# Attention with a gated convolution on one core: V loaded in rows of two tokens, cast by halves of the partitions, masked by a minimum per partition, in a new order of steps

## The chip, the core and the metric

The kernel runs on one core of a Trainium2 chip. The core has five engines that run side by side: TensorE (PE in the profile, its weight loads PEld), VectorE (DVE), ScalarE (ACT), GpSimd (POOL) and SyncE (SP), which here issues nearly all transfers. Sixteen DMA engines move data between the chip's memory and the core's on-chip memory of 128 partitions. The metric is the device time of one execution in microseconds (us); lower is better. Several executions are timed and their median is taken; one execution is profiled.

## What is computed

Eight sequences, eight heads of 64 features, 576 tokens. Attention is causal by blocks of 64 tokens: a query sees all keys of its own block and of those before. Its output x (heads side by side, 512 features) goes through a causal convolution of five taps into a sigmoid gate, through a matrix into values, and gate times values through a second matrix:

```python
scores = scale * np.matmul(q, k.transpose(0, 1, 3, 2))
mask = block_i >= block_j                    # blocks of 64 tokens
attn = softmax(np.where(mask, scores, -1e9))
x = np.matmul(attn, v)                       # then heads side by side
gate = 1.0 / (1.0 + np.exp(-gate_pre))       # gate_pre: conv of x, 5 taps
return gate * (x @ w_val) @ w_out
```

Inputs and output are float32; the kernel works in float16 with float32 sums.

## The kernel before

Work is cut into 32 pairs of heads, four pairs to a batch (a sequence). For each pair, q and k are loaded (L333, rows of 1 KB), cast to float16 (L416, tiles kc and qc), transposed on PE (L441, step T) and evicted into the tile kq (L449 for k, L458 for q). The last 64 tokens of all heads of a batch are a tail with loads, a transpose (L468, step U) and two evictions (L480) of their own. Scores are made with the keys on the partitions, in three steps S for each pair, and ACT takes their exponential into the tile pt (L523, 1,024 columns at a time).

A key tile has 128 keys, two blocks, on the 128 partitions, in the order of the tokens: the earlier block on partitions 0 to 63, the later on 64 to 127. For the queries of the earlier block the later keys must not count, so after the exponential `zeros` (L542) writes zeros into the upper 64 partitions of such columns, on POOL or DVE; `keep_last` (L530) copies the upper half of one block into a small tile pd, where the lower half stays zero.

V is loaded with one token of a head on a partition, 64 floats, 256 B in a row: for the first two batches head by head (L397, `load_head`), then by 128 tokens of all eight heads (L386, `load_v`). Each piece is cast by one instruction of 128x512 (L416) into the tile ve, which has a column of ones beside V for the sums of the softmax. V's tail goes to the upper 64 partitions and is cast there (tile vtail). Step P multiplies pt with ve; DVE takes the reciprocal of the sums (L573) and scales (L583, tile xn). Step X transposes xn on PE, its eviction writes xt (L606); step G is the convolution as matmuls, whose tanh is on ACT (L629); step V is the value matrix, whose product with the gate is on DVE (L651, tile gv); step O is the output matrix, evicted by ACT or DVE (L674, L676) and stored by SP (L684).

No engine's order is left to chance. PE's is a written string, `ORDER`, one letter for each of its 318 steps. For steps that may run on several engines a second string, `CHOICE`, says on which. The class `Planner` then plays the program through with durations, delays between engines and transfer rates from tables, lets each other engine take what it can start earliest, weighed by rank, and so fixes each engine's order; SP's loads of q, k and V follow a fixed list (`queue`). An instruction that waits holds up all that stand behind it on its engine. Where the planner expects PE to be idle in the first 60 us it puts in matmuls of zeros (tile nought, "fillers"). Steps of PE have a mode, by the shape of their matmuls; the planner counts a change between modes with 96 ns, and with about 120 ns an instruction on DVE or POOL that works on the upper partitions after one that does not, or the other way round.

Of the kernel before, what the change touches and what calls it, by code (L numbers as in the profile page):

```python
# [9 lines left out]
SUM_MAX = 60000.0  # L10

# [17 lines left out]
SETUP, SEEN, LANES, SLOTS, SINGLE = 1000, 1400, 8, 2048, 8  # L29

FROM, BUSY, FILL, FULL, NOUGHT = 1050, 9500.0, 60000.0, 4700, (108, 55)


WEIGH = {"PE": 0, "DVE": 83, "ACT": 69, "POOL": 127, "SP": 0}

ORDER = (
    "TTSUSSTSSSTPSSTcXSSSSPPXGPXTXUGVSSVGTGVSVSSVPSVTVPSSXTSVXSSSPGGXPUTGXTSVVGSSVVVS"
    "SVVVSTTPSSPSOXSPSXGXSTTGGSUPSSOXSPSSVVGTTVVSSSVVVVXSTTPSUPXSGGSXPSSOSXOSGGTSVVSS"
    "VVVSUTPPTSOSSVVVSXTPSSOXXGGSSOTSPPSSOXUGGTSVVXTSVVVVSSTPPSSOXSPXGGSXVVVSSTOTUVVS"
    "SSPPGGSTVVSXSVVVSSXPPSTOSSOSTOXXGGGSSTVVVVVVSSSPPPXSGGVVPXXOXGGGVVVVVVVVOOOfOO")  # L40

CHOICE = (
    "DDDADAPPPPDDDPDDDDDPAPDDDDPPPDDADPDADPPDDAAPADPDDDDPDPPDAAADDPPDDPPDADDDPDPPDAAD"
    "PPPADPPDDPPDDDDDPPPDPPPDDAAPPPPADDDDPPPPDPDADDDPDDPPDDPPPPADDPPDDPPPDDADDDDDDPPD"
    "DPDPDDPPDDDDPPDPDAADPPPDAADADPDPDPDDDDPPPPDPPAADDDPDPDDDDDDDAPPAAPDPDDADADPPDPPD"
    "DADPPPPDPDADDPPPAPPDDDPPPADPDDPDPPDDDPDDDDPPDDADPDDDDPPDDDPPDDPPDDDDDPDPPADPPPPA"
    "AAPAAPDPPDDDDPDDDDPPDADDDDDPPDDPPPPAPDADDPPDAAA")
# [15 lines left out]
class Planner:  # L63
# [40 lines left out]
    def plan(self):  # L104
# [3 lines left out]
        bank_free = [0.0] * 7 + [BUSY]  # L108
        mode, dma = None, 0.0
        lands = [0.0] * LANES  # L110
# [33 lines left out]
        def parts(s):  # L144
            rate = s.size[1]
            return s.size[0] / (256 if rate < 250 else 1024 if 300 < rate < 320 else 2048)
# [26 lines left out]
        for left in range(len(self.steps)):  # L173
# [35 lines left out]
            elif s.size:  # L209
                dma = max(dma, s.end + SETUP) + s.size[0] / s.size[1]  # L210
# [19 lines left out]
def kernel(  # L230
# [35 lines left out]
    def ring(n, shape, dtype, name):  # L266
        return [fpool.tile(shape, dtype, tag=f"{name}{i}", name=f"{name}{i}") for i in range(n)]
# [17 lines left out]
    NRAW, NVR, NC, NT, NPT, NX, NXT, NTH, NOB = 3, 5, 4, 8, 4, 3, 3, 8, 4  # L285
    UNIT, TILES = 4, 9
    raws = {n: ring(NRAW, [128, 4, 4, 64], fp32, n + "raw") for n in ("k", "q")}
    vraws = ring(NVR, [128, 8, 64], fp32, "vraw")
# [5 lines left out]
    vtail32 = ring(2, [128, 8, 64], fp32, "vtail32")  # L294
# [3 lines left out]
    KT, K0, Q0 = 128, 192, 704  # L298
# [10 lines left out]
    warm = ring(1, [128, 1], fp32, "warm")[0]  # L309
    ge, both = [raws[n][0][:, :, :, :].rearrange("p e t d -> p (e t d)")[:, 0:NP * 10]  # L310
# [52 lines left out]
    RUN = {1024: 310.0, 256: 200.0, 2048: 330.0, 0: 290.0}  # L363
# [5 lines left out]
    chunks = []  # L369
# [775 lines left out]
```

## Time and profile before

| | before |
|---|---|
| timed runs, median (lowest to highest) | 192.67 us (191.81 to 193.69) |
| the profiled execution, its own time | 193.37 us |
| its span, first to last instruction | 191.4 us |
| PE clock granted | 0.99 |
| bytes moved | 41.02 MB in 64,183 packets, 39,301 of them under 512 B |
| DMA engines' share of busy time on SP's queue | 77.3% of the span |

The span in 40 slices of 4.8 us, as the profile's page draws it (a digit is the busy share in tenths):

```profile
PE   7978999788999989999999999999999999999940
DVE  5468775685978869897989756888977786876020
ACT  3587999497788969799789889688979877743430
POOL 5224451463674615535523546142716001100000
DMA  5999999799869999969999799999981062004291
```

Read the rows against each other: DMA is full from the second slice to the thirtieth, when the last inputs have come; PE has its few gaps in the first seventeen and is full from there to the end. A transfer's price shows in the share of engine time that its packets take, an engine's wait in the idle time before an instruction and in what ended it. The wait is often put down to the engine that ran last, so the reader has to follow it back to what that engine itself had waited for.

### The profile page before, as it was taken

What the parts mean: (1) busy time and instruction counts of PE and PEld (TensorE: products, weight loads), DVE (VectorE), ACT (ScalarE), POOL (GpSimd) and SP (SyncE); (2) the same over time, 40 slices, a digit from 0 to 9 for tenths busy, and PEclk for the clock granted to TensorE, in tenths of its full rate; (3) what the DMA queues carried; (4) which work ended last, traced back from release to release, by engine and by line L of the source; (5) the groups of instructions that cost most, each with busy time, mean ns of one, the idle gap of its engine ahead of it and who ended that gap; (6) DMA issues with size and microseconds to landing.
All of it is one profiled execution on the core that took longest, in us unless ns stands there. A gap on an engine that the chain in (4) does not pass through costs nothing.

```text
span 191.4 us, 9072 instructions
## 1 busy us (share of the span) xinstructions
PE 176.8 (92%) x3898; PEld 130.3 (68%) x3898; DVE 137.6 (72%) x335; ACT 144.1 (75%) x183; POOL 69.4 (36%) x161
## 2 busy tenths in 40 slices
PE   7978999788999989999999999999999999999940
PEld 7766876566676747686686666777688568878430
DVE  5468775685978869897989756888977786876020
ACT  3587999497788969799789889688979877743430
POOL 5224451463674615535523546142716001100000
PEclk9999999999999999999999999999999999999996
DMA  5999999799869999969999799999981062004291
GB/s 152 264 284 306 216 235 340 190 272 198 255 154 263 242 295 262 255 157 322 333 225 270 190 317 288 238 279 281 270 268 47 37 207 92 3 3 113 93 305 56
DMA packets 64183, 41.02 MB, mean 214 GB/s; under 512 B 39301, under 2 KB 58757, under 8 KB 64138
## 3 DMA queue, kind: packets, MB, share of 16 engines
q1 hardware_dynamic: 63562, 39.87, 77.3%
q8 instruction: 32, 0.52, 1.2%
q10 hardware_dynamic: 576, 0.52, 0.9%
q14 instruction: 13, 0.11, 0.2%
HBM read 30.42 MB, written 9.44 MB: 208 GB/s over the span
## 4 chain that ended last, share of the span: by engine, by line
PE 65%; DMA 15%; DVE 9%; ACT 2%; issue 2%; SPq 2%; POOL 0%; ACTq 0%; DVEq 0%; POOLq 0%
PE ps L255 59%; DMA qraw<-in_q_dram 10%; PE ps L441 3%; DMA kraw<-in_k_dram 3%; PE ps L594 3%; DMA tail<-in_q_dram 2%; DVE gv L651 2%; DVE kq L449 1%; DVE w_out L416 1%; ACT kq L458 1%; DVE xn L583 1%; DVE qc L416 1%; SPq L386 1%; DVE kq L458 1%; DVE pd L530 1%
## 5 line engine op out<-in xcount | busy, mean ns | idle before, releaser
L523 ACT ACTIVATE pt<-ps 128x1024 f16<-128x1024 f32 x96 | 94.2, 1025 | 17.3 <-PE ps L255 13.8
L255 PE MATMUL ps<-xt,w_val 128*64 128x288 f16 x512 | 36.3, 288 | 0.0
L255 PE MATMUL ps<-kq 64*128 64x64 f16 (+4 forms) x448 | 33.2, 260 | 1.8 <-DVE kq L480 0.9
L255 PE MATMUL ps<-ve,pt 128*128 128x65 f16 x896 | 33.0, 193 | 1.1 <-issue 0.8
L255 PE MATMUL ps<-w_out,gv 64*128 64x512 f16 (+1 forms) x304 | 33.7, 365 | 0.0
L255 PEld LDWEIGHTS <-pt 128*128 128x128 f16 x896 | 30.1, 97 | 4.0 <-issue 2.1
L651 DVE SCALAR_TENSOR_TENSOR gv<-th,ps 128x288 f16<-128x288 f32 x64 | 27.2, 450 | 6.3 <-PE ps L255 5.3
L255 PEld LDWEIGHTS <-w_val 128*64 128x64 f16 x512 | 27.0, 110 | 5.1 <-issue 2.9
L583 DVE TENSOR_TENSOR xn<-ps,rinv 128x640 f16<-128x640 f32 x32 | 26.4, 824 | 1.1
L255 PEld LDWEIGHTS <-kq 64*128 64x128 f16 x448 | 16.0, 94 | 14.8 <-issue 5.6
L255 PE MATMUL ps<-xt,diag 64*64 64x288 f16 x640 | 23.4, 285 | 0.0
L255 PEld LDWEIGHTS <-gv 64*128 64x128 f16 x304 | 13.8, 94 | 13.2 <-issue 0.2
L629 ACT ACTIVATE th<-ps 128x576 f32<-128x576 f32 x32 | 20.1, 660 | 1.9 <-PE ps L255 1.7
L542 POOL MEMSET pt<- 64x256 f16 x41 | 13.2, 323 | 21.0 <-ACT pt L523 15.5
L255 PEld LDWEIGHTS <-diag 64*64 64x64 f16 x640 | 17.1, 106 | 2.5 <-issue 1.0
L416 POOL CAST qc<-qraw 128x512 f16<-128x512 f32 x22 | 13.6, 629 | 12.6 <-DMA qraw<-in_q_dram 12.1
L416 POOL CAST kc<-kraw 128x512 f16<-128x512 f32 x22 | 13.5, 630 | 12.7 <-DMA kraw<-in_k_dram 10.7
L449 DVE COPY kq<-ps 128x512 f16<-128x512 f16 x19 | 13.1, 690 | 6.9 <-PE ps L441 6.4
L676 DVE TENSOR_SCALAR ob<-ps 128x1024 f32<-128x1024 f32 (+1 forms) x12 | 13.1, 1090 | 3.9 <-PE ps L255 2.3
L255 PE MATMUL ps<-nought 128*128 128x128 f16 x132 | 11.8, 250 | 1.7 <-POOL nought L343 1.0
L674 ACT ACTIVATE ob<-ps 128x1024 f32<-128x1024 f32 (+1 forms) x9 | 8.0, 885 | 6.7 <-PE ps L255 6.7
L573 DVE RECIPROCAL rinv<-ps 128x10 f32<-128x10 f32 x32 | 6.9, 216 | 8.0 <-PE ps L255 7.7
(67 smaller groups left out, 207.4 us busy)
## 6 DMA issues: line engine op xcount, KB each, us to landing
kraw<-in_k_dram SPq DMA_DIRECT2D x12, 512.0 KB, 5.2
qraw<-in_q_dram SPq DMA_DIRECT2D x12, 512.0 KB, 6.5
vraw<-in_v_dram SPq DMA_DIRECT2D x24, 256.0 KB, 6.4
out_dram<-ob SPq DMA_DIRECT2D x11, 512.0 KB, 4.0
kraw<-in_k_dram SPq DMA_DIRECT2D x8, 256.0 KB, 4.3
vraw<-in_v_dram SPq DMA_DIRECT2D x16, 128.0 KB, 5.2
qraw<-in_q_dram SPq DMA_DIRECT2D x7, 256.0 KB, 5.3
out_dram<-ob SPq DMA_DIRECT2D x4, 384.0 KB, 5.7
```

What stands on the lines that cost most here:

```text
L255: nc.tensor.matmul(out=out, lhsT=lhsT, rhs=rhs, start=start, stop=stop, skip_group_check=True)
L416: copier(s.engine)(out=out, in_=in_)
L441: nc.tensor.transpose(out=o, in_=c16[name][rows, t, :, :], identity=ident16[rows, rows])
L449: copier(s.engine)(out=kqs[:, p % NT, K0:K0 + 512].rearrange("p (r s t) -> p r s t", r=2, t=4), in_=ps16[:, i:i + 2, 256:512].rearrange("p ...
L523: nc.scalar.activation(out=heads(p)[:, :, 512 * c:512 * c + 512], in_=ps[:, i:i + 2, :], func=AF.Exp, bias=0.0, scale=0.125)
L542: setter(s.engine).memset(seg[:, :, :, 0:64], 0.0)
L573: nc.vector.reciprocal(out=rinv[:, p, :, :].rearrange("p e (c x) -> p e c x", x=1), in_=o[:, :, :, 64:65])
L583: nc.vector.tensor_tensor(out=xns[p % NX][:, :, :, :].rearrange("p c e d -> p e c d"), in0=o[:, :, :, 0:64], in1=ri.to_broadcast([128, 2, ...
L629: nc.scalar.activation(out=ths[at % NTH][:, 0:n, :, :].rearrange("p n r x -> p (n r) x"), in_=ps[:, i:i + 2 * n, 0:HALF], func=AF.Tanh, bi ...
L651: nc.vector.scalar_tensor_tensor(out=gv[:, 2 * g + r, s0:s0 + HALF], in0=ths[at % NTH][:, n, r, :], scalar=1.0, in1=ps[:, va.group[0], 0:H ...
L674: nc.scalar.activation(out=o, in_=x, func=AF.Copy, bias=0.0, scale=0.5)
L676: nc.vector.tensor_scalar(out=o, in0=x, scalar1=0.5, scalar2=None, op0=ALU.mult)
```

## The change

- A row of V now has two tokens, 512 B. Partition p of a load holds tokens 2p and 2p+1 of a chunk of 256. From the third batch on a batch has two loads of 512 KB instead of four of 256 KB; the buffers are three of 512 KB instead of five of 256 KB.
- The cast puts even tokens on partitions 0 to 63 of a key tile and odd ones on 64 to 127. That takes four casts of 64 partitions for each load: the halves of the load (f) make different key tiles, the halves of the row (u) different partitions. In the first two batches a pair has two steps of two such casts, half as long. V's tail is cast by two instructions of 32 partitions.
- The two blocks of a key tile now alternate in quarters of 32 partitions. The writes that transpose and evict k follow that order. The masks become `tensor_scalar` with a minimum against one of two numbers per partition (tile keep: 65504 or 0), over all 128 partitions.
- The planner gets a rate for rows of 512 B, transfers 7% longer than before, starting times for the first transfers, other weights, and new strings `ORDER` and `CHOICE`.

```diff
-WEIGH = {"PE": 0, "DVE": 83, "ACT": 69, "POOL": 127, "SP": 0}
+WEIGH = {"PE": 0, "DVE": 101, "ACT": 144, "POOL": 117, "SP": 0}
...
-    "TTSUSSTSSSTPSSTcXSSSSPPXGPXTXUGVSSVGTGVSVSSVPSVTVPSSXTSVXSSSPGGXPUTGXTSVVGSSVVVS"
+    "TTUSSTSScSPSTSSSTXPSSPSXPXGGUGXTVGSTVSVSVSSVVSPTVVSXSTSPSSPSXGXUGPTGTXSSVVSSVVVV"
...
-        lands = [0.0] * LANES
+        lands = list(BEFORE)
...
-                dma = max(dma, s.end + SETUP) + s.size[0] / s.size[1]
+                dma = max(dma, s.end + SETUP) + SLOW * s.size[0] / s.size[1]
...
-    RUN = {1024: 310.0, 256: 200.0, 2048: 330.0, 0: 290.0}
+    RUN = {1024: 310.0, 256: 200.0, 512: 265.0, 2048: 330.0, 0: 290.0}
...
     def load_v(b, c):
-            nc.sync.dma_start(out=t[:, :, :],
-                              in_=v[b, :, 128 * c:128 * c + 128, :].rearrange("h p d -> p h d"))
+            nc.sync.dma_start(out=t[:, :, :], in_=v[b, :, 256 * c:256 * c + 256, :].rearrange(
+                "h (p u) d -> p h (u d)", u=2))
...
     def load_head(p, e):
             nc.sync.dma_start(out=t, in_=v[b, 2 * j + e, 0:512, :].rearrange(
-                "(c p) d -> p c d", p=128))
+                "(c p u) d -> p c (u d)", p=128, u=2))
...
+    def spread(key, engines, todo, needs):
+
+        def emit(s):
+            for out, in_ in todo:
+                copier(s.engine)(out=out, in_=in_)
+
+        return add("", key, engines, emit, needs)
...
     def keep_last(p):
-            copier(s.engine)(
-                out=pds[p % NPT][64:128, 0:128].rearrange("p (e x) -> p e x", e=2),
-                in_=heads(p)[64:128, :, 960:1024])
+            setter(s.engine).tensor_scalar(
+                out=pds[p % NPT][:, 0:128].rearrange("p (e x) -> p e x", e=2),
+                in0=heads(p)[:, :, 960:1024], scalar1=keep[:, 1:2], scalar2=None, op0=ALU.min)
...
     def zeros(p, first):
-            setter(s.engine).memset(seg[:, :, :, 0:64], 0.0)
+            seg = seg[:, :, :, 0:64]
+            setter(s.engine).tensor_scalar(out=seg, in0=seg, scalar1=keep[:, 0:1],
+                                           scalar2=None, op0=ALU.min)
...
-            for c in range(4) if b > 1 else ():
+            for c in range(2) if b > 1 else ():
-                chunks.append(copy_step(
-                    p - 1 + 0.1 * c, {"POOL": 613, "DVE": 430, "ACT": 600},
-                    ves[b % 2][:, :, c, 0:64], vraws[(4 * b + c) % NVR][:, :, :],
+                chunks[2 * n] = chunks[2 * n + 1] = [spread(
+                    p - 1 + 0.2 * c, {"POOL": 613, "DVE": 430, "ACT": 600},
+                    [(ves[b % 2][64 * u:64 * u + 64, :, 2 * c + f, 0:64],
+                      vraws[n % NVR][64 * f:64 * f + 64, :, 64 * u:64 * u + 64])],
...
+                    for f in range(2) for u in range(2)]
...
-            chunks.append(copy_step(
-                p - 0.9, {"POOL": 613, "DVE": 430, "ACT": 600},
+            chunks[p] = [spread(
+                p - 0.9, {"POOL": 700, "DVE": 490, "ACT": 660},
+                [(ves[b % 2][64 * u:64 * u + 64, 2 * j:2 * j + 2, f:4:2, 0:64],
+                  vraw(p)[64 * f:64 * f + 64, :, 64 * u:64 * u + 64].rearrange(
+                      "p (e c) d -> p e c d", e=2)) for f in range(2)],
+                P["lv"] + [fill["ve"]]) for u in range(2)]
```

Three places show what the strings and the planner make of it. On SP's queue, the loads of V for the fourth batch, before (tile names carry the number of their buffer, and the last figures are partitions and elements):

```order
L406 DMA vtail_101<-in_v_dram 64x8x64
L386 DMA vraw_85<-in_v_dram 128x8x64
L386 DMA vraw_86<-in_v_dram 128x8x64
L386 DMA vraw_87<-in_v_dram 128x8x64
L684 DMA out_dram<-ob_130 128x2x512
L386 DMA vraw_83<-in_v_dram 128x8x64
L333 DMA kraw_78<-in_k_dram 128x4x256
L333 DMA qraw_81<-in_q_dram 128x4x256
```

and now:

```order
L422 DMA vtail_98<-in_v_dram 64x8x64
L390 DMA vraw_83<-in_v_dram 128x8x128
L390 DMA vraw_84<-in_v_dram 128x8x128
L707 DMA out_dram<-ob_127 128x2x512
L336 DMA kraw_78<-in_k_dram 128x4x256
L336 DMA qraw_81<-in_q_dram 128x4x256
```

Two loads stand where four stood, and the store of an output tile comes behind all of V instead of ahead of its last quarter. On DVE, around the evictions of the fourth batch's tail (L480) before:

```order
L458 COPY kq_106<-ps 128x512
L449 COPY kq_106<-ps 128x512
L458 COPY kq_106<-ps 128x512
L416 COPY kq_106<-kq_106 128x64
L416 CAST ve_105<-vraw_87 128x8x64
L480 COPY kq_106<-ps 128x4x64 x2
L573 RECIPROCAL rinv<-ps 128x10
L583 TENSOR_TENSOR xn_117<-ps,rinv 128x2x5x64
```

and now (L497 and L501 are the evictions of the tail's k and q, L564 a mask, L415 a cast of V):

```order
L629 COPY xt_117<-ps 128x2x5x64
L415 CAST ve_102<-vraw_83 64x8x64
L497 COPY kq_103<-ps 128x4x2x32
L501 COPY kq_103<-ps 128x4x64
L432 COPY kq_103<-kq_103 128x2x32
L415 CAST ve_102<-vraw_84 64x8x64
L596 RECIPROCAL rinv<-ps 128x10
L606 TENSOR_TENSOR xn_114<-ps,rinv 128x2x5x64
L415 CAST ve_102<-vraw_84 64x8x64 x2
L564 TENSOR_SCALAR pt_104<-pt_104,keep_129 128x2x2x64 x2
```

In both a cast of V stands directly ahead of the two evictions; now three more follow soon. On DVE, at the first pairs, before:

```order
L416 COPY kq_106<-kq_106 128x64
L416 CAST ve_104<-vraw_83 128x8x64
L416 CAST kc_90<-kraw_78 128x2x4x64
L416 CAST qc_94<-qraw_81 128x2x4x64
L449 COPY kq_106<-ps 128x512
L458 COPY kq_106<-ps 128x512
L573 RECIPROCAL rinv<-ps 128x10
```

and now:

```order
L432 COPY kq_103<-kq_103 128x2x32
L415 CAST ve_101<-vraw_83 64x4x64 x4
L564 TENSOR_SCALAR pt_104<-pt_104,keep_129 128x2x2x64
L765 COPY convT<-ps 128x20
L432 CAST qc_92<-qraw_81 128x2x4x64
L596 RECIPROCAL rinv<-ps 128x10
```

One cast of V became four, and a mask of the first pair moved onto DVE, ahead of the cast of a later q. In all, DVE has 36 casts of V where it had 13 (20 of them short), POOL 32 for 14 and ACT 12 for 5; ten casts of q and k moved from POOL to DVE and four evictions of tails from DVE to ACT. DVE has 49 masks for 38, POOL 47 for 58. PE has 143 fillers for 132 and 132 changes of mode for 129.

More of the change, by code (lines that the diff above doesn't have):

```diff
@@ L508, in emit @@
                 group(448, 0, 6, 64, stop=False)
-                group(448, KT - 64, 8, 64, start=False)
+                group(448, KT, 8, 64, start=False)
             else:
@@ L794 @@
             done = [pairs[x]["pv"] for x in range(p - 8, p - 4)] if b > 1 else []
-            T["cv"] = copy_step(p - 0.6, {"POOL": 613}, vtails[b % 2][64:128, :, 0:64],
-                                vtail32[b % 2][64:128, :, :], [T["lv"], fill["vtail"]] + done, True)
+            T["cv"] = spread(p - 0.6, {"POOL": 1226},
+                             [(vtails[b % 2][64 * u + 32:64 * u + 64, :, 0:64],
+                               vtail32[64 * (b % 2) + 32 * u:64 * (b % 2) + 32 * u + 32, :, :]) for u in range(2)],
+                             [T["lv"], fill["vtail"]] + done)
         users = before(p - NT, "s0", "s1", "s2")
```

111 lines of the change are left out of this document (62 added, 49 removed).

## The prediction

> **What bounds the kernel now.** I read the page's busy times first, then a table of stretches of the span, then what TensorE (PE) waited for, then the time lines around the longest of those waits, and last the transfers.
>
> ```profile
> PE 176.8 (92%) x3898; PEld 130.3 (68%) x3898; DVE 137.6 (72%) x335; ACT 144.1 (75%) x183; POOL 69.4 (36%) x161
> 25.00:41.00 16.00, 14.07 (x311) 9.31 (x304) 11.19 (x30) 13.26 (x18) 6.26 (x14) 1.00 0.90 254
> 41.00:55.00 14.00, 12.91 (x300) 9.72 (x296) 10.72 (x27) 11.52 (x15) 8.97 (x20) 1.00 0.97 228
> 55.00:83.00 28.00, 26.82 (x642) 19.52 (x639) 23.05 (x56) 23.40 (x31) 13.86 (x30) 1.00 0.97 243
> 83.00:145.00 62.00, 61.77 (x1412) 44.94 (x1412) 50.89 (x117) 52.14 (x64) 26.03 (x58) 1.00 0.96 266
> 145.00:175.00 30.00, 30.00 (x690) 22.92 (x686) 22.28 (x52) 21.80 (x29) 4.55 (x13) 1.00 0.21 63
> ```
>
> A row of stretches has the stretch, its length, busy time (and count) of PE, PEld, DVE, ACT and POOL, the granted clock, the busy share of the DMA engines and GB/s. PE runs at full clock and from 83 us on is idle for 0.23 us in 92: there it is the bound, and its work is the same in both kernels. Between 25 and 83 us it is idle for 1.93 + 1.09 + 1.18 = 4.2 us, and the DMA engines are 90 to 97% busy until 145 us. So there is little to win: those 4.2 us, the fillers ahead of them, and some waits that the modelled ends of matmuls cover. Who makes them:
>
> ```profile
> PE ps L255 <- DVE kq L480: 0.9, 1, 0.9
> PE ps L441 <- DVE qc L416: 0.9, 2, 0.5
> PE ps L255 <- issue: 0.8, 1, 0.8
> PE ps L441 <- POOL kc L416: 0.8, 1, 0.8
> PE ps L441 <- DVE xn L583: 0.7, 1, 0.7
> PE ps L255 <- DVE gv L651: 0.4, 2, 0.2
> ```
>
> Columns: total us, times, longest. The engines named are mostly not the cause. The time lines at 34 and 68 us (start, duration, in brackets the idle time before and its releaser):
>
> ```profile
> 33.55 0.68 PE L255 MATMUL ps<-xt,w_val 128*64 128x288 f16 x8
> 34.98 0.63 DVE L416 CAST qc<-qraw 128x512 f16<-128x512 f32 x1 [1.30 <-DMA qraw<-in_q_dram]
> 35.02 0.29 PE L441 MATMUL ps<-ident,kc 64*128 64x64 f16 x8 [0.80 <-POOL kc L416]
> 35.67 0.29 PE L441 MATMUL ps<-ident,qc 64*128 64x64 f16 x8 [0.36 <-DVE qc L416]
> 39.23 0.29 PE L441 MATMUL ps<-ident,kc 64*128 64x64 f16 x8 [0.67 <-DVE xn L583]
> ...
> 67.72 0.43 DVE L416 CAST ve<-vraw 128x512 f16<-128x512 f32 x1 [1.28 <-DMA vraw<-in_v_dram]
> 68.07 0.75 DVE L480 COPY kq<-ps 128x256 f16<-128x256 f16 x2
> 68.87 0.64 PE L255 MATMUL ps<-kq 64*128 64x448 f16 x12 [0.92 <-DVE kq L480]
> ```
>
> DVE stands 1.30 us at a q cast whose load has not landed, and the xn step behind it makes PE wait again at 39 us. At 68 us DVE stands 1.28 us at a V cast, with the evictions of the tail behind it, for which PE waits. Late loads, not DVE's speed, make these waits.
>
> **The change, part by part.** *Rows of 512 B.* 64 heads of 512 tokens of 256 B are 8.39 MB in 32,768 packets; the change halves the packets. Three stretches in which one packet size filled the engines give the price of a packet (256 B in the last, 1 KB in the first, 2 KB in the middle):
>
> ```profile
> 2.30:4.30 2.00, 2.00 (x20) 1.82 (x18) 1.73 (x13) 1.42 (x2) 0.72 (x5) 1.00 1.00 314
> 28.00:30.00 2.00, 2.00 (x60) 1.31 (x52) 1.02 (x3) 2.00 (x5) 1.21 (x3) 1.00 0.98 355
> 44.20:46.20 2.00, 1.18 (x37) 0.97 (x32) 0.59 (x2) 1.66 (x3) 0.99 (x2) 1.00 1.09 197
> ```
>
> With 16 engines that is 16 x 256 / 197 = 20.8 ns, 16 x 1024 / 314 = 52.2 ns and 92.3 ns a packet. On the line between the first two, 512 B take 31.3 ns, 262 GB/s. V then takes 32.0 us of the engines instead of 42.6: 10.6 less, or 1.26 us for each MB (bounds: 0 at 197 GB/s, 15.9 at 314).
>
> What PE gets of it: ahead of the q load that is late at 35 us stand the heads of six pairs, 1.57 MB, so it lands 2.0 us earlier, more than the 1.30 that DVE waited. Ahead of the V load at 67.7 us stand 2.1 MB of heads and 1.8 MB of batches 2 and 3: 4.9 us, more than 1.28. Both waits go. On PE, counted from start to start against the same step undisturbed:
>
> ```profile
> 27.05 0.68 PE L255 MATMUL ps<-xt,w_val 128*64 128x288 f16 x8
> 27.66 0.81 PE L255 MATMUL ps<-xt,diag 64*64 64x288 f16 x20
> ...
> 32.21 0.60 PE L255 MATMUL ps<-ve,pt 128*128 128x65 f16 x14
> 32.67 0.59 PE L255 MATMUL ps<-ve,pt 128*128 128x65 f16 x14
> 33.22 0.39 PE L255 MATMUL ps<-kq 64*128 64x128 f16 x6
> ```
>
> A V step takes 0.61 us, at 33.55 it took 1.47 until the next: 0.86 lost. The wait at 35.67 costs another 0.36, 0.67 go at 39.23, 0.92 at 68.87, and the gv waits at 80 us (0.4) stand behind a late q cast too. The q wait at 12.5 us (0.5, the other of the two in its row) has one pair's V ahead of it, 0.3 us. Sum 0.86 + 0.36 + 0.67 + 0.92 + 0.4 + 0.3 = 3.5 us saved. The bound below is 0, the bound above the 4.2 idle plus 1.
>
> *Casts by 64 partitions.* From batch 2 on a load has four casts of 64x512 where two loads had one of 128x512 each: 48 for 24. For batches 0 and 1 a pair has four of 64x256 for one. V's tail has two of 32x512 for one.
>
> ```profile
> L416 POOL CAST ve<-vraw 128x512 f16<-128x512 f32 x14 | 8.6, 623 | 0.4
> L416 DVE CAST ve<-vraw 128x512 f16<-128x512 f32 x13 | 5.7, 446 | 1.3 <-DMA vraw<-in_v_dram 1.3
> L416 DVE CAST qc<-qraw 128x512 f16<-128x512 f32 x9 | 4.6, 507 | 3.6 <-DMA qraw<-in_q_dram 3.6
> L416 POOL CAST vtail<-vtail 64x512 f16<-64x512 f32 x8 | 5.0, 629 | 2.9 <-DMA vtail<-in_v_dram 2.0 <-PE ps L441 0.8
> L542 POOL MEMSET pt<- 64x256 f16 x41 | 13.2, 323 | 21.0 <-ACT pt L523 15.5
> L542 DVE MEMSET pt<- 64x128 uint32 x23 | 3.7, 165 | 1.8 <-ACT pt L523 1.3
> L530 DVE COPY pd<-pt 64x128 f16<-64x128 f16 x15 | 3.5, 232 | 2.3 <-ACT pt L523 2.0
> ```
>
> The vtail row shows that 64 partitions take as long as 128 (629 against 623 ns), so a halved cast saves nothing. In the new order DVE has 16 long and 20 short casts for 13: 16 x 0.446 + 20 x 0.27 (an estimate, between 0.22 and 0.446) - 5.7 = +6.8 us. Ten casts of k and q move from POOL to DVE, 10 x 0.47 = +4.7.
>
> *Masks by a minimum.* The trace has no such instruction. On DVE the nearest rows are the memset (165 ns) and the copy of pd (232): I take 200 for 29 + 20 of them, 9.8 us against 3.7 + 3.5, +2.6; at 165 it is +0.9, at the 446 of a cast +14.7. Four tail evictions move to ACT, 0.375 each by the row at 68.07, -1.5. DVE: 6.8 + 4.7 + 2.6 - 1.5 = +12.6 us. POOL has 24 long and 8 short casts of V for 14 (+9 to +10), 8 more of vtail (+5), ten of k and q fewer (-6.3), and 47 minima for 58 masks (from -3 us at a memset's 323 ns to +11 at a cast's 623): about +8 us on an engine at 36%, hidden by its idle time; if that cover is gone, the P steps wait for their masks. ACT takes seven casts and four evictions more, some 4 us on 52.14 of 62 busy in 83:145.
>
> Of these, PE pays where DVE is late without a DMA in front. In 83:145 DVE is busy for 50.9 of 62 us, 82%; a share of the 12.6 us (62 of 169 us) brings it to 89%. At 82% PE lost 0.23 us there. Bounds: 0, and 12.6 if all of it lies on the path. I take 0.8, near the lower end, since that row is the nearest.
>
> *What a rule would make of it.* Around an upper-half mask DVE's pipeline does not overlap:
>
> ```profile
> 13.43 0.69 DVE L449 COPY kq<-ps 128x512 f16<-128x512 f16 x1 [0.46 <-PE ps L441]
> 14.04 0.41 DVE L458 COPY kq<-ps 128x512 f16<-128x512 f16 x1
> 15.59 0.42 DVE L416 CAST ve<-vraw 128x512 f16<-128x512 f32 x1
> 16.04 0.19 DVE L530 COPY pd<-pt 64x128 f16<-64x128 f16 x1
> ```
>
> The second copy starts 0.08 us before the first ends, the mask 0.03 after the cast ends: 0.11 us each way. DVE has 20 runs of such masks; whole-width masks take 40 x 0.11 = 4.4 us of held time away. The Trainium skill (VectorE: DVE Perf Modes, section Two Vector instructions with no wait between them) says that an instruction is held until all earlier ones finish when its input or its output starts in another 32-partition quadrant than the last one's. By that rule the four casts of a group, which start at 0/0, 0/64, 64/0 and 64/64, are held one after the other, some 45 times here, 5 us, and give it all back; without the rule DVE's term would be +8.2 instead of +12.6, and 0.5 on PE instead of 0.8. I leave the 4.4 us out of the sum.
>
> *New order of PE.* The steps are the same. It has 132 changes of matmul mode instead of 129: the P step above takes 0.46 us for its first head and 0.55 for the second with a change behind it, so 0.1 each, +0.3. It has 143 fillers instead of 132, which stand where the plan expects PE idle:
>
> ```profile
> 15.07 1.18 PE L255 MATMUL ps<-nought 128*128 128x128 f16 x18
> ```
>
> 11 of them at 1.18 / 18 us are +0.7. SP issues two V loads a batch instead of four; behind each it comes to k and q sooner, counted above.
>
> **Sum.** -3.5 + 0.8 + 0.3 + 0.7 = -1.7 us. The profiled execution took 193.37 us (span 191.4, so 2.0 outside it), 0.7 above the median of 192.67; 193.4 - 1.7 = 191.7 there. Against the median: 191.0 us, 0.9% less.
>
> **Rivals.** *Bigger gain.* If loads that are early let PE run through 25 to 83 us without any idle time (4.2 for 3.5) and the waits that its records cover (about 1 us) and half of DVE's term go, it is -1.7 - 0.7 - 1 - 0.4 = -3.8, 188.9 us. For it: the DMA share of 0.97 there. Against: the 0.8 of "issue" is no load's.
>
> *Nothing moves.* The casts of the first pairs are four short ones on DVE, and the time won by loads is lost behind them: each group takes 4 x 0.27 against 0.446, 0.6 more, in front of the first P steps; five groups on DVE are 3 us. If half is paid, the sum is -0.2: 192.5. If the change does not do what it says, 512 B packets at 197 GB/s, the 3.5 go and the sum is +1.8: 194.5.
>
> *Slower: one load of 512 KB holds DVE's queue.* Now a cast waits for half as much. If DVE stands in front of a V load with the tail's evictions behind, as at 67.72, and does so in four of the batches 2 to 7, it costs 4 x 1.2 = 4.8 with the rest as summed: +3.1, 195.8 us. It decides from the second such wait on. For it: the order has a V cast directly ahead of both tail evictions on DVE. Against: DMA has 10 us more room.
>
> **How the numbers follow.** Forecast (faster by about 0.9%, 189.6 to 191.9): 0.45. Bigger gain 0.19, nothing moves 0.17, slower 0.19. One per cent, 1.9 us, is about what a measurement of this kernel can tell from no change. Under 190.7 fall the bigger gain and half of the forecast, 0.42; over 194.6 the slower case and little else, 0.20; between them 0.38. The range of 187.8 to 195.2 leaves out the outer part of the two end cases, under 2 in 10.
>
> **What would show it.** Right: the DVE waits for q at 35 us and V at 68 us gone, PE idle between 25 and 83 us under 2 us, loads ended near 135 us instead of 145, under 512 B some 6,500 packets; DVE near 150 us, PE's idle time in 83:145 under 1 us; the minimum at 200 ns on DVE. Wrong: new PE waits for DVE's evictions behind V casts, minima over 300 ns, or a DMA share as before until 145 us.

## The result, and the profile after

The changed kernel takes 199.62 us (median; 199.27 to 203.4) against 192.45 us of the kernel before on the same chip: a ratio of 1.034, 95% interval 1.026 to 1.041. It is slower, and outside the range that was forecast. Some executions of a kernel run a few per cent longer than its others, and the profiled one here is such (203.4 us, span 201.6, against 197.89 to 199.93 for the rest), so its rows say where the time goes, while ratios here and below are those of the other executions.

From the page of the kernel after: busy time by engine, packets, and SP's queue of transfers.

```profile
PE 179.4 (89%) x3909; PEld 131.6 (65%) x3909; DVE 152.3 (76%) x383; ACT 148.8 (74%) x194; POOL 100.9 (50%) x168
...
DMA packets 47607, 41.02 MB, mean 203 GB/s; under 512 B 6341, under 2 KB 42181, under 8 KB 47562
...
q1 hardware_dynamic: 46986, 39.86, 68.4%
```

The rows did their work: 68.4% of 201.6 us are 137.9 us of engine time on SP's queue where 77.3% of 191.4 were 148.0, so 10.1 us less (10.6 were predicted). DVE is busy for 152.3 us (150.2 predicted). POOL is busy for 100.9 us where 69.4 stood before, 31.5 more, and the prediction had written 8.

The stretches of the kernel after (busy time and count of PE, PEld, DVE, ACT, POOL, granted clock, DMA share, GB/s), and what PE waited for:

```profile
25.00:41.00 16.00, 15.07 (x352) 10.94 (x350) 14.28 (x37) 13.26 (x21) 9.75 (x18) 1.00 0.90 278
41.00:55.00 14.00, 12.12 (x296) 9.37 (x297) 12.08 (x28) 12.35 (x18) 11.55 (x17) 1.00 0.89 231
55.00:83.00 28.00, 23.47 (x508) 16.01 (x508) 20.49 (x51) 19.26 (x24) 14.61 (x23) 0.94 0.79 216
83.00:145.00 62.00, 59.42 (x1342) 42.48 (x1338) 52.27 (x120) 51.59 (x66) 41.93 (x66) 1.00 0.86 250
```

```profile
PE ps L257 <- issue: 5.0, 3, 2.6
PE ps L257 <- POOL pt L564: 2.0, 3, 0.8
PE ps L257 <- DVE kq L474: 1.3, 1, 1.3
...
PE ps L257 <- DVE xn L606: 1.0, 2, 0.5
...
PE ps L257 <- DVE pt L564: 0.6, 1, 0.6
```

Between 25 and 83 us PE is idle for 0.93 + 1.88 + 4.53 = 7.3 us where it was 4.2; from 83 to 145 for 2.58 where it was 0.23. Two kinds of wait stand on top: "issue", in which PE waits for nothing that the profile shows (0.8 us before), and the masks (L564, none before).

These sums are those of one execution. The kernel after with V's loads cut in halves takes as long (1.039, see below), and its profile, of a span of 198.8 us, has 4.1 us of idle time between 25 and 83 us and 3.7 from 83 to 145. The same two kinds of wait lead there too:

```profile
PE ps L257 <- issue: 3.8, 4, 1.6
PE ps L257 <- POOL pt L565: 2.5, 4, 0.8
...
PE ps L257 <- DVE pt L565: 0.6, 1, 0.6
```

Against the kernel before that is 3.0 us more for issue and 3.1 for masks, and PE itself is busy for 178.4 us where it was 176.8. Together these are 7.7 us, and the span is 7.4 longer. The masks and casts of the kernel after, by engine and shape:

```profile
L564 POOL TENSOR_SCALAR pt<-pt,keep 128x256 f16<-128x256 f16 x35 | 33.4, 956 | 31.6 <-ACT pt L544 23.0 <-DVE pd L551 6.9 <-PE ps L257 0.9
L415 POOL CAST ve<-vraw 64x512 f16<-64x512 f32 x24 | 15.1, 630 | 1.0
...
L432 POOL CAST kc<-kraw 128x512 f16<-128x512 f32 x18 | 11.0, 623 | 5.0 <-DMA kraw<-in_k_dram 4.8
...
L432 POOL CAST qc<-qraw 128x512 f16<-128x512 f32 x16 | 9.8, 625 | 0.0
L564 DVE TENSOR_SCALAR pt<-pt,keep 128x256 f16<-128x256 f16 x29 | 9.1, 329 | 1.3 <-POOL pd L551 0.6 <-ACT pt L544 0.4
...
L415 DVE CAST ve<-vraw 64x512 f16<-64x512 f32 x16 | 7.8, 489 | 0.3
L551 POOL TENSOR_SCALAR pd<-pt,keep 128x128 f16<-128x128 f16 x12 | 7.6, 637 | 14.5 <-ACT pt L544 14.1
L415 DVE CAST ve<-vraw 64x256 f16<-64x256 f32 x20 | 7.5, 377 | 0.4
...
L551 DVE TENSOR_SCALAR pd<-pt,keep 128x128 f16<-128x128 f16 x20 | 5.8, 289 | 1.4 <-ACT pt L544 1.1
```

A minimum on POOL takes 956 ns for 128x256, and a cast of four times as many bytes of input for twice as many columns (L432) 625. The rows L432 also show that POOL hardly waits for loads any more. Before, its q casts had this row:

```profile
L416 POOL CAST qc<-qraw 128x512 f16<-128x512 f32 x22 | 13.6, 629 | 12.6 <-DMA qraw<-in_q_dram 12.1
```

The 12.1 us in front of the q casts are gone, and of 10.7 in front of the k casts 4.8 are left. Loads that come sooner can do that, and so can a POOL that comes later; the row does not tell the two apart.

### The profile page after: what moved, and what is told of

It is laid out like the page before. It is cut to its first block, busy times and chain, and to the rows that moved or that the text cites. A ratio compares the mean times of both kernels' runs of the same rounds, so it can differ in the third digit from the quotient of the medians.

```text
span 201.6 us, 9115 instructions
## 1 busy us (share of the span) xinstructions
PE 179.4 (89%) x3909; PEld 131.6 (65%) x3909; DVE 152.3 (76%) x383; ACT 148.8 (74%) x194; POOL 100.9 (50%) x168
## 3 DMA queue, kind: packets, MB, share of 16 engines
q1 hardware_dynamic: 46986, 39.86, 68.4%
## 4 chain that ended last, share of the span: by engine, by line
PE 57%; DVE 15%; DMA 11%; issue 5%; ACT 4%; SPq 4%; POOL 1%; DVEq 0%; ACTq 0%; POOLq 0%
PE ps L257 52%; DMA vtail<-in_v_dram 5%; DMA ob<-in_moe_w_val_dram 4%; ACT pt L544 3%; PE ps L457 2%; DVE ve L415 2%; PE ps L617 2%; DVE gv L674 2%; DMA qraw<-in_q_dram 2%; SPq L400 2%; DVE ob L699 1%; DVE kq L465 1%; SPq L336 1%; DVE xn L606 1%; DVE kq L474 1%
## 5 line engine op out<-in xcount | busy, mean ns | idle before, releaser
L564 POOL TENSOR_SCALAR pt<-pt,keep 128x256 f16<-128x256 f16 x35 | 33.4, 956 | 31.6 <-ACT pt L544 23.0
L257 PE MATMUL ps<-ve,pt 128*128 128x65 f16 x896 | 33.9, 194 | 8.1 <-issue 3.7
L257 PEld LDWEIGHTS <-pt 128*128 128x128 f16 x896 | 30.5, 98 | 11.9 <-issue 7.3
L257 PE MATMUL ps<-kq 64*128 64x64 f16 (+4 forms) x448 | 34.4, 263 | 1.2 <-DVE ob L699 0.6
L257 PE MATMUL ps<-w_out,gv 64*128 64x512 f16 (+1 forms) x304 | 34.4, 370 | 0.5 <-DVE xn L606 0.5
L257 PEld LDWEIGHTS <-kq 64*128 64x128 f16 x448 | 16.8, 95 | 13.4 <-issue 5.4
L415 POOL CAST ve<-vraw 64x512 f16<-64x512 f32 (+1 forms) x32 | 18.5, 578 | 1.2
L415 DVE CAST ve<-vraw 64x256 f16<-64x256 f32 (+1 forms) x36 | 15.4, 427 | 0.7
L551 POOL TENSOR_SCALAR pd<-pt,keep 128x128 f16<-128x128 f16 x12 | 7.6, 637 | 14.5 <-ACT pt L544 14.1
L629 DVE COPY xt<-ps 128x640 f16<-128x640 f16 x23 | 11.0, 483 | 3.7 <-PE ps L617 3.6
L432 POOL CAST kc<-kraw 128x512 f16<-128x512 f32 x18 | 11.0, 623 | 5.0 <-DMA kraw<-in_k_dram 4.8
```

The costliest lines, as they stand in the source:

```text
L257: nc.tensor.matmul(out=out, lhsT=lhsT, rhs=rhs, start=start, stop=stop, skip_group_check=True)
L415: copier(s.engine)(out=out, in_=in_)
L432: copier(s.engine)(out=out, in_=in_)
L551: setter(s.engine).tensor_scalar(out=pds[p % NPT][:, 0:128].rearrange("p (e x) -> p e x", e=2), in0=heads(p)[:, :, 960:1024], scalar1=keep ...
L564: setter(s.engine).tensor_scalar(out=seg, in0=seg, scalar1=keep[:, 0:1], scalar2=None, op0=ALU.min)
L629: copier(s.engine)(out=xts[b % NXT][:, g, PAD:PAD + 640].rearrange("p (c r x) -> p r c x", r=2, x=64), in_=ps16[:, i:i + 2, 0:320].rearran ...
```

## The experiments

Theory 1 is the slow minimum on POOL; theory 2 or C, the halved casts; theory 3 or O, the new order; theory F, the waits for issue, taken for late fetches of PE's instructions; theory P, a plan made with wrong durations.

### Parts of the change alone, in the kernel before

*The minimum alone.*

```diff
-                seg = heads(p)[64:128, :, 0:1024].rearrange("p e (s x) -> p e s x", x=512)
+                seg = heads(p)[:, :, 0:1024].rearrange("p e (s x) -> p e s x", x=512)
...
-            setter(s.engine).memset(seg[:, :, :, 0:64], 0.0)
+            seg = seg[:, :, :, 0:64]
+            setter(s.engine).tensor_scalar(out=seg, in0=seg, scalar1=keep[:, 0:1],
+                                           scalar2=None, op0=ALU.min)
```

> The kernel before with one part of the change alone: its masks (the upper 64 partitions, as before) are made by the minimum per partition over 128 partitions, on the engines and in the order of before. Theory 1, the minimum is slow on POOL (956 and 637 ns in the trace after, against 323 and 308 for the memset and the copy): 41 x 0.956 + 17 x 0.637 = 50 us of masks on POOL for 18.4, so POOL is busy some 101 us for 69.4, DVE 142 for 137.6, and P steps and casts on POOL run late: 4 to 7 us slower, 196 to 200 us. Theory 2, the casts by 64 partitions, and theory 3, the new order of steps: within 1% of before.

1.008 (1.003 to 1.014; here and below the ratio to the kernel before on the same chip, with its 95% interval). POOL rose from 69.4 to 99.4 us busy as expected, but of these 30 us only 1.6 came to the kernel's time: theory 1 falls as the whole cause. PE's waits for POOL's masks in it:

```profile
PE ps L255 <- POOL pt L544: 1.3, 3, 0.6
```

*The halved casts alone.*

```diff
-                    ves[b % 2][:, :, c, 0:64], vraws[(4 * b + c) % NVR][:, :, :],
+                    [(ves[b % 2][x:x + 64, :, c, 0:64], vraws[(4 * b + c) % NVR][x:x + 64, :, :])
+                     for x in (0, 64)],
...
```

> The kernel before with the casts of V alone halved as in the kernel after: two casts of 64 partitions for one of 128 (four for the first two batches, half as long), two of 32 for V's tail, on the same engine, in the same place. Theory C: DVE rises by some 7 us busy, POOL by 14, ACT by 3, and 2 to 4 us are lost as whole casts took 3.7 back: 195 to 197 us. Theory O, halved casts cost only where the new order leaves no room: within 1% of before.

1.032 (0.994 to 1.069), a wide interval: the two executions that can be compared took 196.14 and 196.71 us, three of the kernel before 191.27 to 192.94. A loss of some 2% is likely, its size is not settled. DVE is busy for 146.1 us, POOL for 84.2. PE waits for no mask on POOL; its longest sum of waits is now for DVE's product with the gate, 0.4 us before:

```profile
PE ps L255 <- DVE gv L658: 1.8, 2, 1.5
```

*Both.*

> The same with the masks by a minimum as well: all the engine work of the change in the order of before, without the rows of 512 B. If the two costs add (0.8% for the minimum, 1 to 2% for the casts): 196 to 199 us, the kernel after or a little below. If each is hidden in this order: within 1% of before.

1.050 (1.033 to 1.066), 201.18 us: all of the change's work on DVE, ACT and POOL, in the order of before, costs as much as the change itself or more. POOL is busy for 115.1 us, and the masks now make PE wait three times as long as with the minimum alone. The row of PE's waits, then the time line at one of the seven (start, duration; idle time and releaser in brackets):

```profile
PE ps L255 <- POOL pt L551: 3.9, 7, 1.1
```

```profile
69.17 1.45 POOL L424 CAST ve<-vraw 64x512 f16<-64x512 f32 x2
...
70.71 0.97 POOL L551 TENSOR_SCALAR pt<-pt,keep 128x256 f16<-128x256 f16 x1
...
71.73 0.45 PE L255 MATMUL ps<-ve,pt 128*128 128x65 f16 x9 [1.05 <-POOL pt L551]
```

A V cast that is now two, 1.45 us, stands in POOL's queue ahead of a mask that is now 0.97, and the P step waits for both. With either part alone, PE waited 1.3 us or not at all for POOL's masks.

*The rows of 512 B alone.* V's loads read 256 tokens of four heads in place of 128 of eight; sizes, buffers and casts stay.

```diff
-            nc.sync.dma_start(out=t[:, :, :],
-                              in_=v[b, :, 128 * c:128 * c + 128, :].rearrange("h p d -> p h d"))
+            h, x = 4 * (c % 2), 256 * (c // 2)
+            nc.sync.dma_start(out=t[:, :, :].rearrange("p (h u) d -> p h (u d)", u=2),
+                              in_=v[b, h:h + 4, x:x + 256, :].rearrange("h (p u) d -> p h (u d)", u=2))
...
```

> The kernel before with V loaded in rows of 512 B and nothing else changed: pieces of the same size into the same buffers, cast as before, so V's tokens stand at other keys than in the reference. Packets under 512 B fall from 39,301 to about 6,500. The prediction's term: 3.5 us less than before (0 to 5), 188 to 191 us. Theory F by rows: rows in flight make PE's fetches late, issue waits of 2 us or more, 192 to 195 us. Theory O: the issue waits come with the new order, so they stay under 1 us here.

1.006 (1.000 to 1.011): no gain. The waits that the prediction wanted gone are gone, as the idle time in front of DVE's casts of q (3.6 us before) and V (1.3) shows. Others came, in front of DVE's casts of k (0.4 before) and for issue on PE (0.8 before):

```profile
L417 DVE CAST ve<-vraw 128x512 f16<-128x512 f32 x13 | 5.6, 434 | 0.0
L417 DVE CAST kc<-kraw 128x512 f16<-128x512 f32 x10 | 5.5, 552 | 2.5 <-DMA kraw<-in_k_dram 2.4
...
L417 DVE CAST qc<-qraw 128x512 f16<-128x512 f32 x9 | 4.8, 529 | 0.4 <-DMA qraw<-in_q_dram 0.3
```

```profile
PE ps L255 <- issue: 2.3, 3, 1.3
```

In all, PE is idle for 3.5 us between 25 and 145 us where it was 4.4. Nor did the room on the DMA engines bring the loads much earlier. From 49 to 53 us the engines are busy for 0.26 of the time (0.89 before), since SP, by the trace, waits 4.2 us for DVE's cast of w_out (1.1 before), and SP issues the last load at 138.0 us where it was 139.3.

*All but the order.*

> The same rows of 512 B in the kernel before with halved casts and the minimum, which took 5% longer than before: all of the change but its order of steps and its loads of 512 KB. V's tokens stand at other keys than in the reference. If the rows bring what was predicted: 196 to 199 us, the time of the kernel after, and the new order brings nothing. If they are hidden behind the slower masks and casts: 200 us or more.

1.048 (1.039 to 1.056): with the slower masks and casts the rows bring nothing either (1.050 without them). The kernel after stands at 1.034 (1.026 to 1.041), so its new order, larger loads and other placing of keys give back about 1.4%, though the two intervals just touch.

*No masks,* as the base of the next part.

> The kernel before with the masks left out: nothing is written over the scores of later keys and nothing is copied into pd, all other instructions and their order as before. All theories: within 1% of before, since PE waits for a mask for well under 1 us in its trace.

1.001 (0.996 to 1.007).

### Parts of the change undone, in the kernel after

*Masks by memsets and copies again,* two of 32 partitions each.

```diff
-            setter(s.engine).tensor_scalar(out=seg, in0=seg, scalar1=keep[:, 0:1],
-                                           scalar2=None, op0=ALU.min)
+            for a in (32, 96):
+                setter(s.engine).memset(seg[a:a + 32, :, :, 0:64], 0.0)
```

> The kernel after with its masks made as before, by memsets and copies, two of 32 partitions for each minimum, on the same engines and in the same order. Theory 1: POOL falls from 101 us busy to about 90 (70 memsets at 323 ns and 24 copies at 308 are 30 us for 41), DVE rises by some 4 us, and about half of the 7 us lost come back: 195 to 197 us. Theories 2 and 3: no gain, 199 us or more.

A miss: 1.077 (1.066 to 1.088), 207.03 us. A memset of 32 partitions takes as long as one of 64 did (323 and 165 ns):

```profile
L565 POOL MEMSET pt<- 32x256 f16 x70 | 22.2, 317 | 37.1 <-ACT pt L544 21.9 <-DVE pd L552 8.5 <-issue 2.9
...
L565 DVE MEMSET pt<- 32x128 uint32 x58 | 9.6, 165 | 4.4
```

POOL fell to 90.0 us busy as expected, but DVE rose by 9.0 to 161.3 (4 expected), and what PE waits for most is now DVE:

```profile
PE ps L257 <- DVE gv L674: 3.9, 4, 1.9
PE ps L257 <- DVE ob L699: 1.9, 2, 1.2
```

So in this order more work on DVE costs more than less work on POOL gains, and with quarters of 32 partitions the minimum is the cheaper mask.

*No masks.*

> The kernel after with the masks left out in the same way. Theory 1: the whole loss lies in the masks, so it comes to the time of the kernel before without masks or up to 1% below (191 to 193 us). Theories 2 and 3, casts by 64 partitions or the new order: it stays 2 to 3% above the kernel before without masks (196 to 198 us).

1.029 (1.019 to 1.040): nearly all of the loss stays, so it is not the masks by themselves. PE waits for no mask any more, but 5.3 us for issue.

*Whole casts.*

```diff
-                    [(ves[b % 2][64 * u:64 * u + 64, :, 2 * c + f, 0:64],
-                      vraws[n % NVR][64 * f:64 * f + 64, :, 64 * u:64 * u + 64])],
+                    [(ves[b % 2][:, :, 2 * c + f, 0:64],
+                      vraws[n % NVR][:, :, 64 * f:64 * f + 64])] * (1 - u),
```

> The kernel after with V cast by whole instructions: of each pair of casts of 64 partitions the first is made one of 128 partitions and the second is left out, all else in its place. V then stands at other keys than in the reference, the time is that of half the casts. DVE falls by about 8 us busy, POOL by 8 to 9, ACT by 3. Theory C, the halved casts make DVE and POOL late: most of the loss goes, 193 to 196 us. Theories F and O: at most 1.5 us less, 198 us or more.

1.015 (1.005 to 1.024): over half of the loss goes. POOL falls to 91.0 us busy, DVE to 142.3, and PE's waits for issue to 2.4.

*Whole casts and no masks.*

> The kernel after with V cast by whole instructions and without masks: rows of 512 B and the new order alone; V stands at other keys and no mask is made. Theory C with the masks: all of the loss goes, and the rows' gain shows: 190 to 193 us. Theories F and O: 194 us or more, with waits of PE for issue of 2 us or more.

1.028 (1.013 to 1.043), not below the whole casts alone, though POOL is at 51.7 us; the intervals overlap. So with less work on DVE (132.5 us) and POOL than in the kernel before, the rows and the new order still take longer than that kernel. Most of what PE waits for there is issue, 4.4 us in five. In this order the added work is therefore not the whole cause.

*Packets of 256 B again.*

> The kernel after with the rows of 512 B undone alone: V's buffers hold the even and the odd tokens apart, so that each load becomes two with packets of 256 B; casts, masks and order of steps stay. Theory F: PE's own instructions, which the DMA engines fetch in pieces of 16 KB, come late behind loads that are in flight in larger pieces than before (waits of PE for issue 5.0 us after and 5.3 without masks, 0.8 before). Then the issue waits fall to 1.5 us or less and the time to 195 to 198 us, although V takes 10 us more of the DMA engines. Theory C, the work of the halved casts on DVE and POOL, and theory O, the new order: 199 us or more, by up to 3.5 us if the loads' rate was worth what was predicted.

202.97 us in the one execution that can be compared (so no interval for a ratio), a miss for F, which looked for 195 to 198. In the profile, of an execution of 206.07 us, the waits for issue fell to 1.7 us, but PE waits 4.0 us for POOL's masks. That loads which come late in an order made for faster ones are behind this is likely, not shown.

### The waits for issue

In the kernel after the longest lies inside a P step, with all its operands there:

```profile
70.83 0.60 PE L257 MATMUL ps<-ve,pt 128*128 128x65 f16 x14
...
71.30 0.19 PE L257 MATMUL ps<-ve,pt 128*128 128x65 f16 x1
74.11 0.89 PE L257 MATMUL ps<-ve,pt 128*128 128x65 f16 x13 [2.62 <-issue]
```

The view of the transfers between 71.5 and 73 us has one packet of the queue "instruction", 16 KB, and the DMA engines full of loads. Theory F took the wait for PE's own instructions, fetched late behind loads in flight.

*Loads added where DMA is idle,* in the kernel before:

```diff
+        if s.engine == "PE" and s.start > 155000 and not extra:
+            for name, i in (("k", 1), ("q", 1), ("k", 2), ("q", 2))[0:4]:
+                extra.append(load_runs(nc.sync, k, raws[name][i], 0, 2))
```

> The kernel before with four loads of 512 KB more (k and q of the first pairs again, in rows of 1 KB, into buffers of k and q that nothing reads any more), which SP issues at about 160 us, where PE is never idle and the DMA engines carry only stores. Theory F, PE's instructions are fetched behind the loads in flight: 2 MB are some 7 us of the DMA engines at the 300 GB/s of the middle rows; a fetch that is asked for then comes that much later, and PE shows a wait for issue of 1 to 4 us between 155 and 175 us, where it has none now; span 192.5 to 195.5 us. If fetches do not queue behind loads: no issue wait there, span as before (191 to 192), since nothing needs these loads.

> The same with two loads of 512 KB, 1 MB or some 3.5 us. Theory F: the fetch is late by less than PE's store of instructions, so the issue wait is under 0.5 us and the span within 0.6 us of before. If the wait of the other run came from the number of loads or from their rows, it would be half of it here.

One execution of each, 192.75 and 194.33 us, where the kernel before took 192.03 to 193.94. With 2 MB there is one wait for issue in a stretch that had none, with 1 MB none:

```profile
164.53 0.20 PE L594 MATMUL ps<-perm,xn 64*128 64x64 f16 x2 [0.35 <-issue]
```

The direction is F's, the size is not: 0.35 us for the 1 to 4 expected.

The packets' times in the traces settle what these waits are. On the page of the kernel after the larger of the two queues "instruction" (q8) has 32 packets, of 16 KB each, and its 3,909 matmuls are 30.5 times 128. In the 20 traces there are 47 waits for issue of over 0.15 us. When PE's recorded matmuls are counted in groups of 128, each wait stands at the 94th to 96th of a group, and each ends 1.3 to 1.9 us after such a packet has landed. So a packet holds the instructions of 128 matmuls and their weight loads, and where one piece ends and the next has not come, PE waits. In the kernel before such a packet starts in the median 1.8 us after PE has passed the end of a piece while loads run (20 to 140 us), and at once when they are over (146 to 172 us); in the kernel after with halved loads it is 2.4 and 0.3 us. The added 2 MB make one start 2.9 us after the end at 159.1 us, and the wait above follows at the next end. The added 1 MB make it as late, but it lands before PE comes to the next end. Theory F's mechanism is thus shown, and its size, a delay as long as the loads in flight, is not.

*Less in flight.* A limit of 1.1 MB, by a transfer of four bytes that waits for an earlier load, and the same in the kernel before; then V's loads in halves.

```diff
+        if total > 1100000 and s.size[0] >= 131072 and j != at:
+            s.emit = (lambda emit, read, n: lambda x: (
+                nc.sync.dma_start(out=seen[0:1, n:n + 1], in_=read()), emit(x)))(s.emit, loads[j].read, n)
...
```

> The kernel after with a limit on what is in flight: ahead of a load of 128 KB or more SP issues a transfer of four bytes out of the buffer of an earlier load, so that it waits until that load has landed; at most 1.1 MB of loads are then under way (up to 1.9 MB in the trace after without masks). Theory F: the issue waits of PE fall under 1.5 us and the time to 195 to 197 us. Theories C and O: 199 us or more, since nothing lands earlier.

> The kernel before with the same limit of 1.1 MB, as a control for the price of the limit itself. All theories: within 1% of before, its issue waits of 0.8 us or less gone and a load late here and there.

1.150 (1.139 to 1.160) and 1.157 (1.147 to 1.166). There is no wait for issue left in the first, but the limit itself costs 30 us in both, where 1% at most was expected of the control, so the pair decides nothing.

> The kernel after with each 512 KB load of V issued as two of 256 KB, of four heads each, in rows of 512 B as before the split; eight loads may be in flight, so the split lowers the bytes in flight. Theory F: the issue waits fall below 3 us and the time to 196 to 198 us. Theories C and O: no change, 199 us or more.

1.039 (1.032 to 1.046), the kernel after within its interval; 3.8 us of waits for issue. A miss for F's expectation, and loads of half the size do not help.

### The plan

*True durations, old strings.*

```diff
-        P["z0"] = add("", p + 0.4, {"POOL": 400, "DVE": 200}, zeros(p, True), [P["x0"], P["x1"], fill["mask"]])
-        P["z1"] = add("", p + 0.7, {"POOL": 400, "DVE": 200}, zeros(p, False), [P["x2"], P["kl"]])
+        P["z0"] = add("", p + 0.4, {"POOL": 945, "DVE": 300}, zeros(p, True), [P["x0"], P["x1"], fill["mask"]])
+        P["z1"] = add("", p + 0.7, {"POOL": 945, "DVE": 300}, zeros(p, False), [P["x2"], P["kl"]])
...
```

> The kernel after with the planner told what the trace shows for the masks (625 and 945 ns on POOL, 270 and 300 on DVE, for 295, 400, 195 and 200) and for the casts of V; the strings stay, so only the order on POOL, DVE, ACT and SP and the fillers may move. The planner's own end for PE moves from 176.3 to 180.0 us. Theory P, POOL and DVE work in an order that was made for masks of half the length: 2 us or more come back, 195 to 197.5 us. Theory F: within 1.5 us of the kernel after, 198 to 201 us.

1.043 (1.032 to 1.053): no gain. PE has 186 fillers in it where the kernel after has 143; at the prediction's 1.18 us for 18 the 43 more are 2.8 us, an estimate. So this run does not give the price of a wrong plan alone.

*True durations, new strings.*

> The kernel after with the durations that its trace shows (masks and casts, as in the run before with the strings kept) and with strings made anew for them by small changes, each kept where the planner's end came earlier: 96 of the 318 letters of the order and 179 of the 399 choices differ. The planner's end for PE falls from 180.0 us with the old strings to 176.1, 0.6 below that of the kernel before. Theory P, the loss is work that the plan did not know of: with a plan that knows it, PE lags behind the plan as in the kernel before (7.7 us) or as after minus the masks' share (some 10 to 12): 192 to 196 us, the nearest to the kernel before of all versions with rows of 512 B. If halved casts and slow minima cost whatever the order: 198 us or more.

1.011 (1.004 to 1.018), 196.04 us: two thirds of the loss are gone, with as many casts, masks and rows of 512 B. Its masks are no faster, and in PE's waits there is none for a mask:

```profile
L564 POOL TENSOR_SCALAR pt<-pt,keep 128x256 f16<-128x256 f16 x32 | 30.5, 956 | 11.9 <-ACT pt L544 8.6 <-DVE pd L551 1.5 <-DMA kraw<-in_k_dram 0.8
```

```profile
PE ps L257 <- issue: 3.6, 4, 1.5
...
PE ps L457 <- DVE qc L432: 0.5, 1, 0.5
PE ps L257 <- DVE xt L629: 0.5, 1, 0.5
```

POOL is busy for 110.9 us in it, more than the 100.9 of the kernel after, while DVE falls from 152.3 to 149.6 and ACT from 148.8 to 143.6: DVE has 15 of V's casts for 36, POOL 53 for 32. So POOL's load as such does not make the loss; order and choice of engines decide what it costs. That is what theory P said, but the cause is not pinned to the durations: no strings were sought anew with the wrong durations, so a new search alone might have done the same. What is left, 1.1%, is 2.1 us; the waits for issue are 2.8 us above those before. Of the versions that do all of the change's work it is the fastest; it does not beat the kernel before.

## Why the prediction was wrong

**The step that failed first** is the price of the masks on POOL, and that they cost PE nothing: "47 minima for 58 masks (from -3 us at a memset's 323 ns to +11 at a cast's 623): about +8 us on an engine at 36%, hidden by its idle time". The masks on POOL came to 33.4 + 7.6 = 41.0 us for 18.4, +22.6, twice the upper end, and POOL's whole term to +31.5: a cast is no upper bound for a minimum with a number per partition, though it has twice the columns. Nor was it hidden. The new work alone, in the order of before, takes 5.0% more time, with 3.9 us of waits for POOL's masks. The sentence behind it, "if that cover is gone, the P steps wait for their masks", is what happened there, but no rival was made of it. In the kernel after, in its other order, the masks are the smaller part: without them the ratio falls from 1.034 to 1.029 only, with whole casts to 1.015. The planner was told 400 ns, and the prediction compared its own price with neither the plan's durations nor what a wrong one does to an order that is fixed by them.

**The step that failed second** is "-3.5" for late loads. The waits at q and V went, also in the kernel before with the rows alone; but that kernel measured 1.006 (1.000 to 1.011), no gain. The sum counted each wait of PE as won when its load came earlier. In the run PE's idle time fell by 0.9 us, since other waits (issue 2.3 us for 0.8) took their place, and part of the DMA engines' room went unused behind SP's queue. The sign "loads ended near 135 us" did not come either: SP issued the last load at 145.6 us in the kernel after, 139.3 before.

**A term put at nothing** is the waits for issue. The prediction held that "the 0.8 of "issue" is no load's" and left it as it was. It is a fetch of PE's instructions that comes late while loads run, and these waits grew to 5.0 us (3.8 with V's loads in halves).

**DVE's term** (+0.8 on PE for 12.6 us more work) had the sum of the work nearly right, 152.3 us for 150.2, and that is partly luck. The masks on DVE came to 14.9 us for 7.2, +7.7 where +2.6 was written, and the casts of V to 15.3 for 5.7, +9.6 for +6.8. The sum fits all the same through rows that it did not count, such as 14 evictions of k on DVE for 19. The minimum on DVE took 329 and 289 ns where 200 was taken and "over 300" was named as a sign of being wrong. Its share on PE was too low: whole casts, which relieve DVE by 10.0 us and POOL by 9.9, took the ratio from 1.034 to 1.015. How much of that is DVE's was not tried; the memsets, with 9.0 us more on DVE and 10.9 less on POOL, went from 1.034 to 1.077.

**The rule on held instructions** (the Trainium skill, VectorE: DVE Perf Modes, section Two Vector instructions with no wait between them) agrees with this trace: of the casts of V that follow each other on DVE in the kernel after, each begins 13 to 31 ns after the end of the last (18 pairs); in the kernel before with halved casts and the minimum, where two of four work on the same partitions, those begin 74 to 82 ns before it (8 pairs). That is about 0.1 us a pair, 1.7 us in all, where 5 were worked out for 45.

**The rivals.** Slower had 0.19, by one load of 512 KB in front of DVE's tail evictions. PE waits for neither of these evictions (L497, L501) in the kernel after, and V's loads in halves did not help (1.039): the rival's outcome came, but not by its mechanism. The terms for modes and fillers (+0.3, +0.7) were not tried apart; PE is busy 1.6 us longer with V's loads in halves than before.

**Open:** why the waits for issue are longer in most kernels with the new order (2.4 to 5.3 us). The rows alone do not set it: without them the kernel before without masks has 1.8 us, and with them and the new order the kernel with memsets has 0.8. One reading fits all these traces and was not tried by itself: a late fetch costs only what is left of it when PE gets there, so whatever else holds PE up hides it, and what is taken away brings it out. Without masks they are 5.3 us, without masks and with whole casts 4.4; with the memsets, where PE waits for DVE, 0.8, and with the limit on loads none. That would also be why taking out parts gave back so little.

## What to carry to other kernels

An engine at 36% is no cover for work whose price has not been measured: what counts is its queue, and a cast that became two in front of a mask that became three times as long made PE wait for masks three times as long as with the slower mask alone. In a kernel whose order is planned from a table of durations, a new operation's true duration belongs in the table before its order is judged; here that, together with a search for new strings, was worth two thirds of the loss. Transfers that need 10 us less of the DMA engines gave no gain in a kernel whose TensorE was busy for 92% of the span. And a wait that is taken away is not yet time won: look at what stands right behind it.

## What was not expected of the hardware

A minimum with a number per partition takes 956 ns for 128x256 and 637 for 128x128 on POOL, against 329 and 289 on DVE; that is 2.5 ns a column, where POOL's cast of 128x512 took 625 in all. On POOL memsets and copies of 32 partitions cost as much as those of 64 (317 ns for 323, 312 for 308), and so do memsets on DVE (165 for 165). And PE can stand up to 2.62 us inside a step with all its operands there, every 128 matmuls, when the 16 KB with its next instructions come late behind loads.
